# All attention scores of a head pair in one TensorE batch, two more jobs that ScalarE may take, and new TensorE prices in the planner

## The chip, the cores and the metric

One core of a Trainium2 chip. The metric is the device time of one launch in microseconds (us). The kernel before took 643.71 us, median of three runs (640.93 to 644.32). Engines in the profile: PE is TensorE's matmuls, PEld its weight loads, DVE is VectorE, ACT ScalarE, POOL GpSimd, SP the queue that issues the DMAs.

## The reference, cut to what matters

```python
# q, k, v: (2, 8, 768, 64) f32; n_sink = 4, window = 128
scores = q @ k.T / sqrt(64)
keep   = (key < n_sink) | (0 <= query - key < window)
a      = softmax(where(keep, scores, -1e9))
x      = (a @ v), heads side by side          # 1536 tokens x 512
h = maximum(x @ moe_w_in, 0);  x = (h * h) @ moe_w_out        # 512 -> 2048 -> 512
h = x @ moe2_w_in;  out = (h * sigmoid(1.702 * h)) @ moe2_w_out
```

Everything is float32, and n_sink and window are data that the kernel reads.

## The kernel before, in words

**Attention.** Queries go in 6 groups of 256 and, in each, 4 pairs of heads: 24 pairs, one call of `Attn.pair` each. A group has four blocks of 64 queries; block n sees 128 + 64 keys of its window and 8 sink keys, `KB` = 200 columns. `pair` goes over w = 0 and 1 (two blocks each). For each w, `mm_quarters` (L397) issues the scores as 64x64 tiles of the TensorE array, two blocks by two heads, into columns 0 to 200 of the PSUM banks a0 and a1 (one per head). Then, per head, VectorE adds the mask and takes the maximum (L765), and ScalarE takes the exponential with its sum (L767). The batch of w = 1 writes the same columns as that of w = 0, so it waits until VectorE has read both banks. In the first group of a batch element the batch of w = 0 has 136 columns (`cuts`). The transposes (L418) of the probabilities, the product with v as 128x64 or 64x64 tiles (`mm_halves`, L411) and two more transposes make a slice of x, which is split into a high and a low float32r part.

**The two layers.** Each goes over 16 blocks of 128 hidden units and over 3 tiles of 512 tokens (in attention's time, over 256 tokens: groups 0 to 3, three blocks of layer 1). A step is `first` (12 matmuls, L392), `act`, `second` (12 matmuls). For 512 tokens that is 24 matmuls of 512 columns. In layer 1 `act` has ScalarE take the relu of the PSUM bank into r (L564), VectorE multiply the bank by r in place (`tt`, L369), ScalarE copy it into gh (L351) and VectorE subtract gh (L369).

**Weights.** They arrive as 64-bit words and are decoded in pieces of 128x512, two for each of 32 blocks (`decode`). A piece takes on VectorE a range check (L479: the smallest absolute value, kept in a column of `least`), two shifts and masks (L482, L487), two combinations (L483, L489) and a mask (L491); on ScalarE a scaling (L485) and a copy (L351); and a multiplication on VectorE or GpSimd (L369, L370). 11 blocks are kept in SBUF: 7 from the start, 4 more when attention has given back its space. `make_flag` tests `least` at the end.

**The order.** Nothing is issued in the order of the text. Every operation is added to a `Plan` with a price in ns, what it reads and what it writes, and with a price for each engine that may take it (`choose`). `solve` plays six rounds of a list schedule with these prices, with `LAG` between engines, a model of TensorE's clock (`Clock`) and weights per engine (`PRICE`, ScalarE 1.2 and VectorE 1.5 per ns), keeps the shortest, and `emit` writes the instructions in that order. On the chip each engine then works through its own list in order. While there is nothing else for TensorE at the start, the plan puts matmuls of zeros there (L857).

Of the kernel before, what the change touches and what calls it, by code (L numbers as in the profile page):

```python
# [9 lines left out]
F32 = mybir.dt.float32  # L10
# [274 lines left out]
def kernel(  # L285
# [59 lines left out]
    def in_psum(*aps):  # L345
        return any(t.space == bass.MemoryType.PSUM for t in aps)
# [19 lines left out]
    def tt(engs, o, a, b, op, reads=(), writes=(), wide=0):  # L366
        n = o.free_size()
        every = {
            "V": ((100 if in_psum(a, b) else 69) + 1.04 * n, lambda: nc.vector.tensor_tensor(o, a, b, op)),  # L369
            "P": (145 + (2.11 + wide) * n, lambda: nc.gpsimd.tensor_tensor(o, a, b, op)),  # L370
        }
        ps = in_psum(o, a, b)
        choose([e for e in engs if not (e == "P" and ps)], every, not in_psum(a, b), reads, writes)
# [4 lines left out]
    def vec(ns, fn, reads=(), writes=(), port=False):  # L378
        step("V", ns, fn, reads, writes, port=port)
# [7 lines left out]
    def mm(calls, reads, writes):  # L387


        def fn():  # L390
            for o, a, b, start, stop in calls:
                nc.tensor.matmul(o, a, b, start=start, stop=stop)  # L392

        ns = lambda n, dt: max(107, (1 if dt == F32R else 4) * n / 2.4 + 2.5)
        step("E", sum(ns(c[2].free_size(), c[2].dtype) for c in calls), fn, reads, writes, calls[0][1].shape[0] / P)

    def mm_quarters(calls, n, reads, writes):  # L397


        def fn():  # L400
            for o, a, b, start, stop in calls:
                nc.tensor.matmul(o, a, b, start=start, stop=stop)  # L402

        step("E", 4 * n / 2.4 + 70, fn, reads, writes, 0.8)

    def mm_halves(calls, reads, writes):


        def fn():
            for o, a, b, start, stop in calls:  # L410
                nc.tensor.matmul(o, a, b, start=start, stop=stop)  # L411

        step("E", sum(2 * c[2].free_size() / 2.4 + 8 for c in calls) + 60, fn, reads, writes, 0.8)

    def transposes(calls, reads, writes):
        def fn():
# [8 lines left out]
    lim = T(cpool, [P, 2], F32, "lim")  # L425
    lim_hi = T(cpool, [P, 2], F32, "lim_hi")
    ns_f, win_f = lim[:, 0:1], lim[:, 1:2]
    least = T(cpool, [P, 4 * NF], F32, "least")
    flag_f = T(cpool, [P, 3], F32, "flag_f")
    flag_i = T(cpool, [P, 1], I32, "flag_i")  # L430

# [10 lines left out]
    def make_flag():  # L442

        a, b = flag_f[:, 0:1], flag_f[:, 1:2]

        def fn():
            nc.vector.tensor_scalar(a, ns_f, float(NS), None, ALU.is_gt)
            nc.vector.tensor_scalar(b, win_f, 1.0, None, ALU.is_lt)
            nc.vector.tensor_tensor(a, a, b, ALU.max)
            nc.vector.tensor_scalar(b, win_f, float(P), None, ALU.is_gt)  # L450
            nc.vector.tensor_tensor(a, a, b, ALU.max)
            nc.vector.tensor_reduce(b, least, AX.X, ALU.min)
            nc.vector.tensor_scalar(b, b, LEAST_HI, None, ALU.is_lt)
            nc.vector.tensor_tensor(a, a, b, ALU.max)

        def last():
            nc.vector.tensor_reduce(flag_f[0:1, 2:3], banks["a2"][0:1, 0:P], AX.X, ALU.max)
            nc.vector.tensor_copy(flag_i[0:1], flag_f[0:1, 2:3])

        vec(900, fn, ["lim", "least"], ["flag"])  # L460
        transposes([(banks["a2"][0:1, 0:P], a)], ["flag"], ["a2"])
        vec(400, last, ["a2"], ["flag"])


    def decode(raw, rk, w, wk, least_col, scratch, keep):

        words = raw.bitcast(I32).rearrange("p (n t) -> p n t", t=2)  # L470
        lo, hi = words[:, :, 0], words[:, :, 1]
        kl, kh = (rk, "lo"), (rk, "hi")
        a, ka = scratch()
        if keep is not None:
            vec(600, lambda: nc.vector.tensor_scalar(a, hi, 0x7FFFFFFF, None, ALU.bitwise_and), [kh], [ka])
            vec(600, lambda: nc.vector.tensor_scalar(keep, fv(a), LEAST_HI, None, ALU.is_ge), [ka], ["keep"])
            tt("V", fv(hi), fv(hi), keep, ALU.mult, [kh, "keep"], [kh])
        else:
            vec(602, lambda: nc.vector.tensor_reduce(least_col, fv(hi), AX.X, ALU.min, apply_absolute_value=True),  # L479
                [kh], ["least"])  # L480

        vec(335, lambda: nc.vector.tensor_scalar(lo, lo, 9, None, ALU.logical_shift_right), [kl], [kl], True)  # L482
        vec(602, lambda: nc.vector.scalar_tensor_tensor(lo, hi, 23, lo, ALU.logical_shift_left, ALU.bitwise_or),  # L483
            [kh, kl], [kl], True)
        act(520, lambda: nc.scalar.activation(fv(lo), lo.bitcast(U32), AF.Copy, scale=2.0**-43), [kl], [kl])  # L485

        vec(335, lambda: nc.vector.tensor_scalar(a, hi, 0x07FFFE00, 3, ALU.bitwise_and, ALU.logical_shift_left),  # L487
            [kh], [ka], True)
        vec(602, lambda: nc.vector.scalar_tensor_tensor(a, hi, -0x40000000, a, ALU.bitwise_and, ALU.bitwise_or),  # L489
            [kh, ka], [ka], True)  # L490
        vec(335, lambda: nc.vector.tensor_scalar(hi, a, -0x800000, None, ALU.bitwise_and), [ka], [kh], True)  # L491
        copy(EN["dH"], w[0], fv(a), [ka], [(wk, "h")])
        tt(EN["dL"], w[1], fv(lo), fv(hi), ALU.mult, [kl, kh], [(wk, "l")], wide=0.3)


    class Moe:
# [25 lines left out]
        def decode(self):  # L522

            if self.n_dec == len(self.blocks):
                return
            blk = self.blocks[self.n_dec]
            t, wk = self.weights[self.n_dec % len(self.weights)]
            for mat in range(2):
                raw, rk = self.raw()
                dma(raw, w_dram[(blk[0], mat)][blk[1]], (), [(rk, "lo"), (rk, "hi")])  # L530
                n = 2 * self.n_dec + mat
                col = least[:, n : n + 1] if self.check else None
                decode(raw, rk, t[2 * mat : 2 * mat + 2], (wk, mat), col, self.scratch, self.keep)
            self.w[blk] = (t, wk)
            self.n_dec += 1

# [21 lines left out]
        def act(self, s):  # L558
# [6 lines left out]
            else:  # L565
                act(51 + 0.833 * n, lambda: nc.scalar.activation(r, ps, AF.Sigmoid, scale=GELU), [bank, "table"], [kr])  # L566

            tt("V", ps, ps, r, ALU.mult, [kr, bank], [bank])
            copy(EN["gh"], gh, ps, [bank], [kh])
            sub("V", gl, ps, fv(gh), [bank, kh], [kl])  # L570
            s["g"] = (gh, gl, kh, kl)
# [124 lines left out]
    class Attn:  # L696
# [27 lines left out]
        def pair(self, i):  # L724
# [13 lines left out]
            p, pk = self.p()  # L738
            st, stk = self.st()
            nm, sm, ri = (st[:, 4 * n : 4 * n + 4] for n in range(3))  # L740
            for w in range(2):
                cut = cuts[w]
                mask, mask_keys = self.masks[(first, w)]

                if w == 0:
                    parts = [(cut, KB - cut, [K_AT[u] + cut for u in range(2)])]
                else:
                    parts = [(0, P, [K_AT[u] + WIDE_AT[u] for u in (2, 3)]),
                             (P, KB - P, [K_AT[u] + REST_AT[u] for u in (2, 3)])]
                calls = []  # L750
                for dst, n, src in parts:
                    for b in range(2):
                        for h in range(2):
                            q = Q0 + (2 * w + b) * P + h * HQ
                            calls.append((
                                banks[BANKS["s"][h]][half(b), dst : dst + n], raw[half(h), q : q + HQ],
                                raw[half(h), K0 + src[b] : K0 + src[b] + n], True, True,
                            ))
                mm_quarters(calls, KB - cut, [(rk, "qk")], list(BANKS["s"]))
                for h in range(2):  # L760
                    n, one = KB - cut, slice(2 * w + h, 2 * w + h + 1)
                    pu = p[:, 2 * w + h, cut:]

                    vec(77 + 1.04 * n, lambda pu=pu, ps=banks[BANKS["s"][h]][:, cut:KB], mask=mask[:, cut:], one=one:
                        nc.vector.tensor_tensor_reduce(pu, ps, mask, -0.125, 3.0e38, ALU.add, ALU.min, nm[:, one]),  # L765
                        [BANKS["s"][h]] + mask_keys, [(pk, w, h), (stk, "nm", w, h)])
                    act(280 + 0.833 * n, lambda pu=pu, one=one: nc.scalar.activation(  # L767
                        pu, pu, AF.Exp, bias=nm[:, one], scale=-1.0, accum_out=sm[:, one]),
                        [(pk, w, h), (stk, "nm", w, h)], [(pk, w, h), (stk, "sm", w, h)])
# [54 lines left out]
    with ExitStack() as fast:  # L824
# [31 lines left out]
        early[0] = True  # L856
        plan[0].filler = lambda: nc.tensor.matmul(banks["h"][:, 0:P], zero, zero, start=True, stop=True)  # L857
        vec(100, lambda: nc.vector.memset(zero, 0.0), (), ["zero"])
        at.load()
        constants()  # L860
        at.masks = build_masks(sums[NTILE - 1].rearrange("p a b -> p (a b)"))
# [195 lines left out]
```

## Time and profile before

| | |
|---|---|
| median of the runs | 643.71 us |
| the profiled execution | 644.05 us, its span 642.1 us |
| PE busy | 625.8 us, 97% of the span |
| DVE / ACT / POOL busy | 445.2 (69%) / 281.1 (44%) / 35.3 us (6%) |
| mean granted clock of TensorE | 0.989 of full |

Busy shares are means over the span, and the kernel has two parts: attention with a little of layer 1 up to about 156 us, and the two layers alone after that. Matmuls overlap, so a matmul's "busy" is longer than its pace. What one costs where TensorE has a queue of work is the distance between the starts of neighbours.

### The profile page before, as it was taken

The page shows a single profiled execution, that of the slowest core. Times are in us where ns is not written, and L with a number is a line of the kernel's source. Part 1 is how long each engine was busy: PE and PEld are TensorE (multiplying, and loading weights), DVE is VectorE, ACT ScalarE, POOL GpSimd, SP SyncE. Part 2 cuts the span into 40 slices and gives each one's busy share as a digit, 9 for nine tenths or more (in the row PEclk, how much of TensorE's full clock was granted, in tenths as well). Part 3 has the DMA queues.
Part 4 walks back from the last instruction along what each step waited for, and adds up shares of the span by engine and source line. Part 5 has one row for each costly group of instructions (what it writes and reads, how often), then busy time and mean ns, then how long its engine had stood idle before and what let it go on. Part 6 is the DMA issues. An engine that isn't in the chain of part 4 may idle for free.

```text
span 642.1 us, 10443 instructions
## 1 busy us (share of the span) xinstructions
PE 625.8 (97%) x4039; PEld 517.2 (81%) x4039; DVE 445.2 (69%) x1040; ACT 281.1 (44%) x626; POOL 35.3 (6%) x45
## 2 busy tenths in 40 slices
PE   7999999998999999999999999999999999999995
PEld 6777778897888888888888888888888888888884
DVE  5898889988877889998888998522277651333313
ACT  4687677764533444353343544232444331221211
POOL 1010000001010010010020110000000000000000
PEclk7999899999999999999999999999999999999998
DMA  6686655323122112241131312100021200101001
GB/s 241 200 267 222 222 187 187 121 69 129 66 98 100 61 70 86 79 132 52 57 123 34 98 38 94 34 1 0 5 94 66 84 16 1 65 1 65 1 0 70
DMA packets 14744, 56.77 MB, mean 88 GB/s; under 512 B 1760, under 2 KB 1760, under 8 KB 14688
## 3 DMA queue, kind: packets, MB, share of 16 engines
q1 hardware_dynamic: 14688, 56.04, 26.2%
q8 instruction: 33, 0.54, 0.4%
q14 instruction: 23, 0.19, 0.1%
HBM read 52.89 MB, written 3.15 MB: 87 GB/s over the span
## 4 chain that ended last, share of the span: by engine, by line
PE 94%; DVE 2%; ACT 1%; DMA 1%; issue 0%; SPq 0%; ACTq 0%
PE c L392 41%; PE a L392 25%; PE h L392 15%; PE c L411 5%; PE a L402 3%; PE c L418 3%; PE a L418 2%; DMA ints<-in_limits_dram 1%; PE h L857 1%; DMA raw<-in_w_out_dram 1%; ACT p L767 0%; DVE sum L369 0%; ACT pw L351 0%; DVE pw L352 0%; DVE p L765 0%
## 5 line engine op out<-in xcount | busy, mean ns | idle before, releaser
L392 PE MATMUL a<-xh,w 128*128 128x512 f32 x480 | 156.9, 390 | 0.0
L392 PE MATMUL c<-w,ghw 128*128 128x512 f32 x384 | 118.4, 389 | 0.0
L392 PE MATMUL c<-ghw,w 128*128 128x512 f32 x336 | 107.2, 389 | 2.0 <-ACT ghw L351 2.0
L392 PEld LDWEIGHTS a<-xh,w 128*128 128x128 f32 x480 | 90.1, 188 | 18.7
L392 PE MATMUL h<-xh,w 128*128 128x512 f32 (+1 forms) x336 | 104.7, 366 | 0.0
L369 DVE TENSOR_TENSOR a<-a,rw 128x512 f32<-128x512 f32 x60 | 41.9, 698 | 76.4 <-ACT rw L566 65.2
L392 PE MATMUL a<-xl,w 128*128 128x512 f32 x240 | 93.4, 389 | 0.0
L392 PEld LDWEIGHTS c<-w,ghw 128*128 128x128 f32 x384 | 72.0, 188 | 15.0
L392 PEld LDWEIGHTS c<-ghw,w 128*128 128x128 f32 x336 | 63.1, 188 | 15.4 <-ACT ghw L351 2.5
L392 PE MATMUL c<-w,glw 128*128 128x512 f32 x192 | 74.7, 389 | 0.0
L392 PEld LDWEIGHTS h<-xh,w 128*128 128x128 f32 x336 | 62.3, 190 | 9.8 <-issue 0.3
L392 PE MATMUL c<-glw,w 128*128 128x512 f32 x168 | 65.5, 390 | 0.2 <-DVE glw L369 0.2
L485 ACT ACTIVATE raw<-raw 128x512 f32<-128x512 uint32 x64 | 43.2, 675 | 43.2 <-DVE raw L483 43.1
L392 PE MATMUL h<-xl,w 128*128 128x512 f32 (+1 forms) x168 | 60.5, 360 | 0.0
L369 DVE TENSOR_TENSOR glw<-a,ghw 128x512 fp32r<-128x512 f32 x60 | 41.2, 687 | 17.7 <-ACT ghw L351 16.6
L351 ACT ACTIVATE ghw<-a 128x512 fp32r<-128x512 f32 x60 | 36.0, 599 | 39.0 <-DVE a L369 35.0
L566 ACT ACTIVATE rw<-a 128x512 f32<-128x512 f32 x32 | 19.2, 599 | 76.9 <-PE a L392 76.5
L392 PEld LDWEIGHTS a<-xl,w 128*128 128x128 f32 x240 | 45.1, 188 | 9.2
L351 ACT ACTIVATE w<-dec 128x512 fp32r<-128x512 f32 x64 | 40.2, 631 | 19.8 <-DVE dec L489 17.2
L479 DVE TENSOR_REDUCE least<-raw 128x1 f32<-128x512 f32 x64 | 43.3, 677 | 6.8 <-DMA raw<-in_w_out_dram 6.6
L767 ACT ACTIVATE p<-p,st 128x200 f32<-128x200 f32 (+1 forms) x96 | 42.5, 448 | 7.4 <-DVE st L765 7.0
L370 POOL TENSOR_TENSOR w<-raw 128x512 fp32r<-128x512 f32 x21 | 22.8, 1087 | 411.8 <-DVE raw L491 300.4
(101 smaller groups left out, 907.1 us busy)
## 6 DMA issues: line engine op xcount, KB each, us to landing
raw<-in_w_in_dram SPq DMA_DIRECT2D x32, 512.0 KB, 3.9
raw<-in_w_out_dram SPq DMA_DIRECT2D x32, 512.0 KB, 3.5
qkv<-in_qkv_dram SPq DMA_DIRECT2D x16, 840.0 KB, 4.7
qkv<-in_qkv_dram SPq DMA_DIRECT2D x7, 680.0 KB, 5.2
out_dram<-sum SPq DMA_DIRECT2D x12, 256.0 KB, 2.1
qkv<-in_qkv_dram SPq DMA_DIRECT2D x1, 424.0 KB, 3.4
qkv<-in_qkv_dram SPq DMA_DIRECT2D x1, 256.0 KB, 6.8
ints<-in_limits_dram SPq DMA_DIRECT2D x1, 2.0 KB, 3.9
```

The lines of the kernel that those rows point to most:

```text
L351: "A": ((51 if ps else 94) + 0.833 * n, lambda: nc.scalar.activation(o, i, AF.Copy)),
L369: "V": ((100 if in_psum(a, b) else 69) + 1.04 * n, lambda: nc.vector.tensor_tensor(o, a, b, op)),
L370: "P": (145 + (2.11 + wide) * n, lambda: nc.gpsimd.tensor_tensor(o, a, b, op)),
L392: nc.tensor.matmul(o, a, b, start=start, stop=stop)
L402: nc.tensor.matmul(o, a, b, start=start, stop=stop)
L411: nc.tensor.matmul(o, a, b, start=start, stop=stop)
L418: nc.tensor.transpose(o, i, ident)
L479: vec(602, lambda: nc.vector.tensor_reduce(least_col, fv(hi), AX.X, ALU.min, apply_absolute_value=True), [kh], ["least"])
L485: act(520, lambda: nc.scalar.activation(fv(lo), lo.bitcast(U32), AF.Copy, scale=2.0**-43), [kl], [kl])
L566: act(51 + 0.833 * n, lambda: nc.scalar.activation(r, ps, AF.Sigmoid, scale=GELU), [bank, "table"], [kr])
L767: act(280 + 0.833 * n, lambda pu=pu, one=one: nc.scalar.activation(pu, pu, AF.Exp, bias=nm[:, one], scale=-1.0, accum_out=sm[:, one]), [(p ...
L857: plan[0].filler = lambda: nc.tensor.matmul(banks["h"][:, 0:P], zero, zero, start=True, stop=True)
```

## The change

- `pair` issues the scores of w = 0 and w = 1 in one batch (`mm_quarters` is called once, with 24 matmuls). Those of w = 1 go to columns 200 to 400 of the same banks. VectorE's four reads follow.
- `decode`'s range check may go to ScalarE: the absolute value into a scratch tile `junk`, then relu(LEAST_HI - |x|), whose sum is kept in a column of `below`. The plan chooses by price, 602 ns on VectorE or 1130 ns on ScalarE. `least` and `below` are set by GpSimd at the start, and `make_flag` tests `below` with three more VectorE instructions.
- In layer 1 the square may go to ScalarE: Square of r into the bank, for VectorE's multiplication of the bank by r.
- Prices: a matmul of n columns costs n/2.4 + 13.4 ns (before n/2.4 + 2.5), a score batch 180 ns beside its columns (before 70), a product with v 190 ns (before 60), a VectorE `tensor_tensor` 74 + 1.04n ns.

```diff
 def tt(...):
-            "V": ((100 if in_psum(a, b) else 69) + 1.04 * n, lambda: nc.vector.tensor_tensor(o, a, b, op)),
+            "V": (74 + 1.04 * n, lambda: nc.vector.tensor_tensor(o, a, b, op)),
 def mm(...):
-        ns = lambda n, dt: max(107, (1 if dt == F32R else 4) * n / 2.4 + 2.5)
+        ns = lambda n, dt: max(107, n / 2.4 + 13.4 if dt == F32R else 4 * n / 2.4 + 5)
 def mm_quarters(...):
-        step("E", 4 * n / 2.4 + 70, fn, reads, writes, 0.8)
+        step("E", 4 * n / 2.4 + 180, fn, reads, writes, 0.8)
 def mm_halves(...):
-        step("E", sum(2 * c[2].free_size() / 2.4 + 8 for c in calls) + 60, fn, reads, writes, 0.8)
+        step("E", sum(2 * c[2].free_size() / 2.4 + 8 for c in calls) + 190, fn, reads, writes, 0.8)
 def make_flag(): ...
+            nc.vector.tensor_reduce(b, below, AX.X, ALU.max)
+            nc.vector.tensor_scalar(b, b, 0.0, None, ALU.is_gt)
+            nc.vector.tensor_tensor(a, a, b, ALU.max)
 def decode(...):
-            vec(602, lambda: nc.vector.tensor_reduce(least_col, fv(hi), AX.X, ALU.min, apply_absolute_value=True),
-                [kh], ["least"])
+            def by_scalar():
+                nc.scalar.activation(junk, fv(hi), AF.Abs)
+                nc.scalar.activation(junk, junk, AF.Relu, bias=least_hi, scale=-1.0, accum_out=below_col)
+            every = {
+                "V": (602, lambda: nc.vector.tensor_reduce(least_col, fv(hi), AX.X, ALU.min, apply_absolute_value=True)),
+                "A": (1130, by_scalar),
+            }
+            choose("VA", every, False, [kh, "checks"], ["check"])
 def act(self, s):
-            tt("V", ps, ps, r, ALU.mult, [kr, bank], [bank])
+            every = {"V": (74 + 1.04 * n, lambda: nc.vector.tensor_tensor(ps, ps, r, ALU.mult))}
+            if s["layer"] == 1:
+                every["A"] = (69 + 0.833 * n, lambda: nc.scalar.activation(ps, r, AF.Square))
+            choose(list(every), every, False, [kr, bank], [bank])
 def pair(self, i):
+            for w, dst, n, src in (
+                (0, cuts[0], KB - cuts[0], [K_AT[u] + cuts[0] for u in (0, 1)]),
+                (1, 0, P, [K_AT[u] + WIDE_AT[u] for u in (2, 3)]),
+                (1, P, KB - P, [K_AT[u] + REST_AT[u] for u in (2, 3)]),
+            ):
+                for b in range(2):
+                    for h in range(2):
+                        q = Q0 + (2 * w + b) * P + h * HQ
+                        calls.append((
+                            banks[BANKS["s"][h]][half(b), w * KB + dst : w * KB + dst + n], raw[half(h), q : q + HQ],
+                            raw[half(h), K0 + src[b] : K0 + src[b] + n], True, True,
+                        ))
+            mm_quarters(calls, 2 * KB - cuts[0], [(rk, "qk")], list(BANKS["s"]))
             for w in range(2):
-                ...
-                mm_quarters(calls, KB - cut, [(rk, "qk")], list(BANKS["s"]))
                 for h in range(2):
-                    vec(77 + 1.04 * n, lambda pu=pu, ps=banks[BANKS["s"][h]][:, cut:KB], mask=mask[:, cut:], one=one:
+                    vec(77 + 1.04 * n, lambda pu=pu, ps=ps, mask=mask[:, cut:], one=one:
                     ...
+        def checks():
+            nc.gpsimd.memset(least, 1.0e30)
+            nc.gpsimd.memset(below, 0.0)
+            nc.gpsimd.memset(least_hi, LEAST_HI)
+        step("P", 450, checks, (), ["checks"])
```

## Rows read from the trace of the kernel before

**Rows 1.** The page: busy us, share and instructions by engine; granted clock in 40 slices.

```profile
PE 625.8 (97%) x4039; PEld 517.2 (81%) x4039; DVE 445.2 (69%) x1040; ACT 281.1 (44%) x626; POOL 35.3 (6%) x45
PEclk7999899999999999999999999999999999999998
```

**Rows 2.** Windows: stretch, its length, busy us of each engine, PEclk, DMA, GB/s.

```profile
14.00:75.50 61.50, 59.20 (x946) 46.81 (x944) 54.75 (x215) 46.29 (x158) 3.13 (x3) 1.00 0.67 217
75.50:79.00 3.50, 3.50 (x29) 3.12 (x19) 2.15 (x8) 1.51 (x6) 0.00 (x0) 0.53 0.72 253
79.00:146.00 67.00, 66.59 (x857) 56.86 (x857) 59.33 (x199) 47.67 (x141) 4.51 (x4) 1.00 0.43 148
146.00:156.00 10.00, 7.73 (x39) 6.09 (x38) 8.54 (x18) 5.87 (x13) 2.04 (x2) 1.00 0.23 63
156.00:632.60 476.60, 476.60 (x2104) 394.64 (x2104) 310.12 (x555) 173.79 (x290) 23.47 (x23) 1.00 0.17 57
632.60:642.10 9.50, 2.06 (x10) 1.36 (x8) 2.73 (x4) 0.00 (x0) 0.00 (x0) 0.83 0.33 118
```

**Rows 3.** Waits of PE from 14 to 156 us: us in total, times, longest.

```profile
PE c L392 <- ACT ghw L351: 2.0, 1, 2.0
PE c L411 <- DVE xl L369: 1.7, 3, 1.0
PE c L418 <- ACT p L767: 0.4, 1, 0.4
PE c L392 <- DVE glw L369: 0.2, 1, 0.2
```

**Rows 4.** Timeline of PE around three score batches (L402): start, us, instruction, count.

```profile
52.90 0.57 PE L402 MATMUL a<-qkv 64*64 64x200 f32 x8
53.40 0.44 PE L418 MATMUL c<-ident,xn 128*128 128x128 f32 x2
...
54.60 0.28 PE L392 MATMUL h<-xl,w 128*128 128x256 f32 x1
54.71 0.28 PE L392 MATMUL h<-xh,w 128*128 128x256 f32 x1
54.92 0.57 PE L402 MATMUL a<-qkv 64*64 64x128 f32 x16
55.43 0.34 PE L411 MATMUL c<-qkv,pr 72*64 72x64 f32 x4
...
71.30 0.46 PE L402 MATMUL a<-qkv 64*64 64x136 f32 x8
71.69 0.30 PE L418 MATMUL c<-ident,p 128*72 128x128 f32 x1
```

**Rows 5.** Lines by form, whole span: busy us, mean ns, idle before, releaser.

```profile
L479 DVE TENSOR_REDUCE least<-raw 128x1 f32<-128x512 f32 x64 | 43.3, 677 | 6.8 <-DMA raw<-in_w_out_dram 6.6
L369 DVE TENSOR_TENSOR h<-h,r 128x256 f32<-128x256 f32 x12 | 5.1, 429 | 1.3 <-ACT r L564 1.2
L485 ACT ACTIVATE raw<-raw 128x512 f32<-128x512 uint32 x64 | 43.2, 675 | 43.2 <-DVE raw L483 43.1
L351 ACT ACTIVATE w<-dec 128x512 fp32r<-128x512 f32 x64 | 40.2, 631 | 19.8 <-DVE dec L489 17.2 <-PE c L392 2.4
L767 ACT ACTIVATION_READ_ACCUMULATOR p<-p,st 128x1 f32 x96 | 18.5, 193 | 0.0
L564 ACT ACTIVATE r<-h 128x256 f32<-128x256 f32 x12 | 4.6, 380 | 7.0 <-PE h L392 7.0
L882 ACT ACT_TABLE_LOAD x1 | 1.3, 1283 | 0.0
```

**Rows 6.** The chain that ended last, 146 to 156 us: start, us, what.

```profile
146.42 3.41 DMA raw<-in_w_out_dram
...
151.22 0.59 DVE least L479
...
152.41 0.60 DVE least L479
```

More of the change, by code (lines that the diff above doesn't have):

```diff
@@ L427 @@
     ns_f, win_f = lim[:, 0:1], lim[:, 1:2]
-    least = T(cpool, [P, 4 * NF], F32, "least")
+    least, below = (T(cpool, [P, 4 * NF], F32, tag) for tag in ("least", "below"))
+    least_hi = T(cpool, [P, 1], F32, "least_hi")
+    junk = T(cpool, [P, DM], F32, "junk")
     flag_f = T(cpool, [P, 3], F32, "flag_f")
@@ L458, in last, with decode @@
             nc.vector.tensor_copy(flag_i[0:1], flag_f[0:1, 2:3])
-        vec(900, fn, ["lim", "least"], ["flag"])
+        vec(1300, fn, ["lim", "check"], ["flag"])
         transposes([(banks["a2"][0:1, 0:P], a)], ["flag"], ["a2"])
         vec(400, last, ["a2"], ["flag"])
-    def decode(raw, rk, w, wk, least_col, scratch, keep):
+    def decode(raw, rk, w, wk, least_col, below_col, scratch, keep):
         words = raw.bitcast(I32).rearrange("p (n t) -> p n t", t=2)
@@ L531, in decode @@
                 n = 2 * self.n_dec + mat
-                col = least[:, n : n + 1] if self.check else None
-                decode(raw, rk, t[2 * mat : 2 * mat + 2], (wk, mat), col, self.scratch, self.keep)
+                decode(raw, rk, t[2 * mat : 2 * mat + 2], (wk, mat), least[:, n : n + 1], below[:, n : n + 1],
+                       self.scratch, self.keep)
             self.w[blk] = (t, wk)
@@ L740, in pair @@
             nm, sm, ri = (st[:, 4 * n : 4 * n + 4] for n in range(3))
+            calls = []
+            for w, dst, n, src in (
[11 more added lines that the diff above has]
+            mm_quarters(calls, 2 * KB - cuts[0], [(rk, "qk")], list(BANKS["s"]))
             for w in range(2):
@@ L743, in pair @@
                 mask, mask_keys = self.masks[(first, w)]
[L745 to L758, printed above, removed]
-                mm_quarters(calls, KB - cut, [(rk, "qk")], list(BANKS["s"]))
                 for h in range(2):
                     n, one = KB - cut, slice(2 * w + h, 2 * w + h + 1)
-                    pu = p[:, 2 * w + h, cut:]
-                    vec(77 + 1.04 * n, lambda pu=pu, ps=banks[BANKS["s"][h]][:, cut:KB], mask=mask[:, cut:], one=one:
+                    pu, ps = p[:, 2 * w + h, cut:], banks[BANKS["s"][h]][:, w * KB + cut : (w + 1) * KB]
+                    vec(77 + 1.04 * n, lambda pu=pu, ps=ps, mask=mask[:, cut:], one=one:
                         nc.vector.tensor_tensor_reduce(pu, ps, mask, -0.125, 3.0e38, ALU.add, ALU.min, nm[:, one]),
```

## The prediction, made before the changed kernel was run

> **What bounds the kernel now.** I read the page's engine table and clock first, then windows, then TensorE's waits, then its timeline around single batches, and the prices of lines last. The table says TensorE 97%, VectorE 69% [rows 1], but that is a mean over two different parts, so the windows count [rows 2]. From 156.0 to 632.6 us TensorE runs 2104 matmuls in 476.6 us, 226.5 ns each, with no gap: only fewer or cheaper matmuls would shorten that stretch, and the change alters none of them. VectorE has 310 of 477 us there and ScalarE 174, so work that moves between these two is hidden behind TensorE in that part, at nothing; the cover is 167 us of idle VectorE and 303 us of idle ScalarE. The last 9.5 us are the last matmuls, four VectorE sums and the stores; nothing in the change touches them. What is left is the part before 156 us.
>
> There TensorE is also the one with a queue of work. From 14 to 146 us (the first three windows) VectorE is busy 54.75 + 2.15 + 59.33 = 116.2 of 132 us (88%) and ScalarE 46.29 + 1.51 + 47.67 = 95.5 us (72%) [rows 2]. TensorE's own waits from 14 to 156 us add up to only 2.0 + 1.7 + 0.4 + 0.2 = 4.3 us [rows 3]. So in attention TensorE's issue time sets the pace, with VectorE close behind, and TensorE time that goes there comes off the end. Two losses stand beside it: 3.4 us at half clock (0.53 of full in 75.5 to 79.0, that is 1.2 in place of 2.4 GHz), 2 us after TensorE's longest wait for VectorE (1.0 us, [rows 3]), which costs 1.7 us; and 146 to 156 us, where TensorE is busy 7.7 of 10 us.
>
> **The change part by part.**
>
> *One batch in place of two.* The price of a batch comes from three of them [rows 4]. A batch of 200 columns starts at 52.90 and the next instruction at 53.40: 0.50 us. One of 136 columns takes from 71.30 to 71.69: 0.39 us. So 64 columns cost 0.11 us, 1.72 ns a column; 200 columns stream in 0.344 us, and 0.156 us of a batch is fixed. The batch of w = 1, which has its 200 columns in 16 matmuls of 128 and 72 columns, takes 54.92 to 55.43, 0.51 us: more matmuls within the same tiling cost 0.01, so the fixed part belongs to the batch and not to its matmuls. Getting in costs too: matmuls of 256 columns stand 0.11 apart (54.60, 54.71), but 0.21 before the batch (54.71, 54.92), so 0.10 more. Each batch less saves 0.156 + 0.095 = 0.25 us. There are 24 pairs with one batch less each: 24 x 0.25 = 6.0 us. Bounds: 0.16 us if the entry is hidden by a longer queue (3.7 us), and 0.3 if the pause for the banks goes too (7.2 us); I take 6.0, the measured sum.
>
> *The wait for the banks.* Today the batch of w = 1 waits for two reads by VectorE and the next pair's first batch for two more; afterwards one batch waits for four. What is queued behind a waiting batch on TensorE is all that the plan put after it: transposes, products with v and layer matmuls. The loop is then about 1.0 us of batch, four reads of at most 0.43 us (VectorE's 256-column form [rows 5]) and two hand-overs, about 3 us, against (146 - 14) / 24 = 5.5 us of a pair's period today, so it does not bind. Value: nothing; up to 0.1 us a pair (2.4 us) lost if the plan puts the batch too close behind the reads, up to the 1.7 us of waits for VectorE gained.
>
> *The range check.* On VectorE 0.677 us a piece [rows 5]; 22 pieces belong to the 11 blocks decoded by about 156 us, 14.9 us. ScalarE's form isn't in the trace. The nearest rows: the absolute value reads the same strided words as L485 (0.675), the relu is like L351 from SBUF (0.631), its sum read-out like L767's (0.193): 1.50 us, against 1.13 in the plan; as a low bound the plan's 1.13. All 22 would put ScalarE at 95.5 + 33 = 128.5 us in a stretch of 126: they cannot all go. The plan weighs 1.2 x 1130 = 1356 against 1.5 x 602 = 903, so ScalarE gets a check only where it could begin 0.45 us earlier. I take a third, 7: VectorE -4.7, ScalarE +10.5 us.
>
> *The square.* VectorE 0.429 us on 256 columns, ScalarE about the 0.380 of its relu [rows 5]; of 12 in attention I take half: VectorE -2.6, ScalarE +2.3. Together VectorE has 116.2 - 4.7 - 2.6 = 109 and ScalarE 95.5 + 10.5 + 2.3 = 108 us in 126, 87% each: they remain under TensorE. If nothing moved, VectorE would be at 116 / 126 = 92%. The rows alone make ScalarE the dearer engine for the check (1.50 against 0.677) and the cheaper one for the square (0.380 against 0.429). The Trainium skill speaks against both: "ScalarE: Activation LUTs" (Rules for kernel authors) wants relu and multiplications on VectorE and not on ScalarE; the rows agree for the check and not for the square, and what it would cost here is a rival below.
>
> *The prices.* The new price of a 512-column matmul, 512/2.4 + 13.4 = 226.7 ns, is what the trace has (226.5); the old one gave 215.8. The plan now knows TensorE's pace and the 0.25 us around a batch. That orders the other engines' work by later and truer due times. Of the 4.3 us of waits I count 1 us as gone, with bounds of +4 (a new order with waits of its own) and -4.3 us. The wait at the end of attention is the largest (2.0 + 0.2): the chain there goes from a weight DMA of 3.41 us through the decoding on VectorE, two range checks of 0.6 us among it [rows 6], to the first 512-column step; two checks on ScalarE would take up to 1.2 us off it.
>
> *Small parts.* Three more instructions for the flag and three GpSimd memsets lie in time that these engines idle (POOL has 35 us of work in the whole span); nothing. At the start, the second scores come sooner, but their masks don't: nothing, within 1 us either way. The half-clock stretch I leave as it is: 1.7 us to gain if TensorE waits less, as much to lose if a wait comes elsewhere.
>
> **Sum.** Span 642.1 - 6.0 - 1.0 = 635.1; the profiled execution took 1.95 us more than its span, so 637.0. That execution (644.05) stands 0.3 above the median of 643.71, so against the median I say 637.0 as well, 6.7 us or 1.0% less. The likeliest case's own range: 633.5 to 640.4.
>
> **The rivals.**
>
> *VectorE takes over* (0.19). Its 116 us of work, in order, have 16 us of idle in 132, and if these are unavoidable hand-overs, VectorE keeps the pace, and TensorE's 6 us turn into waits: 641 to 646, 644 in the middle. For it: the longest waits of TensorE are on VectorE [rows 3]. Against it: they are short and few, and both new choices can only take work off VectorE.
>
> *ScalarE in the way* (0.10, slower). ScalarE works in order, and a check of 1.5 us, priced at 1.13, in front of an exponential delays the transposes, the product with v and the next layer step. From 0.25 x 24 / 1.5 = 4 checks of the 22 that lie fully on TensorE's path the gain is gone; with 8 it is 644 + 6 = 650. Against it: 28% of ScalarE is idle in that stretch. The rule of the Trainium skill cited above points to this case.
>
> *A table for Square* (0.04, slower). A table load takes 1.283 us, and the line that brings in the sigmoid's has one [rows 5]; if Square or Abs needed another table than the exponential, 12 squares in attention would bring up to 24 loads, 31 us on ScalarE: 95.5 + 31 is more than the stretch, some 5 us over, so about 644 + 5 = 649. The Trainium skill, "ScalarE: Activation LUTs" (Table sets: the hidden batching unit), names relu, copy, identity and abs as filler of every set, and not Square; no row here shows a Square.
>
> *The plan clears its waits* (0.12). Batches 6.0, waits 4.3, the half clock 1.7: 632 and below to about 630. The chain of 146 to 156 us speaks for it, the fixed order on engines with jitter against it.
>
> **How the numbers follow.** Forecast 0.55. A change of under 0.5% (3.2 us) can't be told from none here: faster means below 640.5, slower above 646.9. Faster: 0.55 + 0.12 = 0.67; same: 0.19; slower: 0.10 + 0.04 = 0.14. The range of 631.5 to 645.5 takes the forecast's own, half of the case below it and most of VectorE's: about 0.8.
>
> **What would show it.** One score batch of 24 matmuls a pair, lasting about 2 x 0.344 + 0.16 = 0.85 us to the next instruction, 24 of them in place of 48. The stretch without gaps then begins about 149 us in place of 156, at 226.5 ns a matmul as before. VectorE's share before it falls, ScalarE's rises; some checks (an Abs and a Relu) and Squares appear on ScalarE, with no further table load. Wrong would be: a batch of 1.1 us (the fixed part went with the columns); the saving turned into waits for VectorE or ScalarE before 150 us; gaps after it; or the batches back at two.

## The result, and the profile after

The changed kernel takes 637.65 us (median of 7 runs, 636.66 to 639.38), the kernel before, run beside it, 644.32 us (640.93 to 645.7): ratio 0.9903, 95% interval 0.988 to 0.9925. Forecast: 637.0, in 631.5 to 645.5. The profiled span went from 642.1 to 635.7 us, 6.4 us less.

The page after (engines and granted clock, as in [rows 1]):

```profile
PE 619.5 (97%) x4033; PEld 516.8 (81%) x4033; DVE 401.6 (63%) x974; ACT 343.8 (54%) x771; POOL 36.8 (6%) x50
...
PEclk8999999999999999999999999999999999999998
```

Windows of the kernel after, columns as in [rows 2]; the first four answer to the first four there:

```profile
14.00:75.50 61.50, 59.29 (x970) 51.01 (x968) 56.86 (x227) 53.39 (x174) 3.12 (x3) 1.00 0.66 228
75.50:79.00 3.50, 3.50 (x54) 3.02 (x46) 3.33 (x14) 2.78 (x10) 0.00 (x0) 1.00 0.88 322
79.00:146.00 67.00, 64.36 (x813) 57.26 (x809) 57.81 (x186) 55.70 (x156) 8.57 (x7) 1.00 0.46 155
146.00:156.00 10.00, 10.00 (x46) 8.29 (x45) 7.02 (x15) 6.95 (x13) 0.00 (x0) 1.00 0.39 137
...
128.60:144.30 15.70, 13.63 (x103) 11.59 (x103) 12.34 (x24) 11.84 (x25) 3.43 (x3) 1.00 0.31 102
144.30:626.10 481.80, 480.70 (x2112) 395.56 (x2111) 274.53 (x501) 226.54 (x411) 22.00 (x21) 1.00 0.17 55
626.10:635.70 9.60, 2.92 (x13) 2.07 (x12) 2.84 (x5) 0.00 (x0) 0.00 (x0) 0.78 0.33 118
```

The long stretch of layers begins at 144.3 us in place of 156, and the last part is as long as before (9.6 against 9.5 us). From 75.5 to 79.0 us the clock is now at full. VectorE's total fell by 43.6 us and ScalarE's rose by 62.7: the checks that moved are dearer on ScalarE.

Two score batches of the kernel after (timeline of PE, the rows that answer to [rows 4]): one with 200 columns for w = 0 and one with 136. The trace has two records for each float32 matmul, so the 24 of a batch are the 12 matmuls that the program issues.

```profile
119.97 0.28 PE L392 MATMUL h<-xh,w 128*128 128x256 f32 x1
120.09 0.60 PE L418 MATMUL c<-ident,p 128*72 128x128 f32 x4
120.52 0.60 PE L418 MATMUL a<-ident,p 128*128 128x128 f32 x4
121.05 0.91 PE L402 MATMUL a<-qkv 64*64 64x200 f32 x24
121.89 0.34 PE L411 MATMUL c<-qkv,pr 72*64 72x64 f32 x4
...
16.73 0.81 PE L402 MATMUL a<-qkv 64*64 64x136 f32 x24
17.46 0.44 PE L418 MATMUL c<-ident,xn 128*128 128x128 f32 x2
```

From 121.05 to 121.89 is 0.84 us, for which two batches took 0.50 + 0.51, and one entry of 0.10 is gone as well. The median over the 24 batches is 0.843 us, measured from a batch's first matmul to the next instruction's; of the 48 before it was 0.504.

TensorE's waits in the whole kernel after (us, times, longest; [rows 3] are those of before up to 156 us):

```profile
PE a L402 <- DMA qkv<-in_qkv_dram: 3.3, 3, 2.4
PE c L392 <- ACT ghw L351: 2.0, 2, 1.7
PE h L872 <- DVE zero L873: 1.1, 1, 1.1
PE c L392 <- DVE glw L369: 1.1, 4, 0.4
PE c L411 <- DVE xl L369: 1.1, 3, 0.5
```

One is new: score batches that wait for the DMA of q, k and v, 2.4 us of it at the start, the rest in attention.

What ScalarE took over up to 146 us, and the checks that stayed on VectorE (L490) (lines by form: busy us, mean ns | idle before):

```profile
L487 ACT ACTIVATE junk<-junk,least_hi 128x512 f32<-128x512 f32 x9 | 6.5, 723 | 0.4
L490 DVE TENSOR_REDUCE least<-raw 128x1 f32<-128x512 f32 x9 | 6.1, 681 | 1.0 <-DMA raw<-in_w_out_dram 1.0
L486 ACT ACTIVATE junk<-raw 128x512 f32<-128x512 f32 x9 | 6.1, 680 | 3.7 <-DMA raw<-in_w_out_dram 2.1 <-DMA raw<-in_w_in_dram 1.6
L583 ACT ACTIVATE h<-r 128x256 f32<-128x256 f32 x10 | 3.8, 384 | 0.2
L487 ACT ACTIVATION_READ_ACCUMULATOR junk<-junk,least_hi 128x1 f32 x9 | 1.7, 186 | 0.0
L351 ACT ACT_TABLE_LOAD x1 | 1.3, 1283 | 0.7 <-PEq L1069 0.7
L904 ACT ACT_TABLE_LOAD x1 | 1.3, 1283 | 0.0
```

Nine checks of 0.680 + 0.723 + 0.186 = 1.59 us and ten squares of 0.384 us; two table loads in all, as before.

### The profile page after: what moved, and what is told of

Its sections match the earlier page's. It is cut to its first block, busy times and chain, and to the rows that moved or that the text cites. A ratio compares the mean times of both kernels' runs of the same rounds, so it can differ in the third digit from the quotient of the medians.

```text
span 635.7 us, 10424 instructions
## 1 busy us (share of the span) xinstructions
PE 619.5 (97%) x4033; PEld 516.8 (81%) x4033; DVE 401.6 (63%) x974; ACT 343.8 (54%) x771; POOL 36.8 (6%) x50
## 4 chain that ended last, share of the span: by engine, by line
PE 61%; DVE 17%; DMA 14%; ACT 5%; issue 2%; POOL 1%; SPq 0%; DVEq 0%; POOLq 0%; ACTq 0%
PE c L392 27%; PE a L392 16%; PE h L392 9%; DMA raw<-in_w_out_dram 8%; PE c L411 3%; DMA qkv<-in_qkv_dram 3%; DMA raw<-in_w_in_dram 3%; PE a L402 2%; DVE raw L496 2%; DVE dec L502 2%; PE c L418 2%; DVE glw L369 1%; DVE raw L495 1%; DVE sum L369 1%; DVE dec L500 1%
## 5 line engine op out<-in xcount | busy, mean ns | idle before, releaser
L392 PE MATMUL a<-xh,w 128*128 128x512 f32 x480 | 158.8, 389 | 0.0
L392 PE MATMUL c<-ghw,w 128*128 128x512 f32 x336 | 108.5, 390 | 1.7 <-ACT ghw L351 1.7
L392 PE MATMUL h<-xh,w 128*128 128x512 f32 (+1 forms) x336 | 103.4, 363 | 0.0
L581 DVE TENSOR_TENSOR a<-a,rw 128x512 f32<-128x512 f32 x40 | 27.9, 697 | 65.1 <-ACT rw L579 64.9
L502 DVE SCALAR_TENSOR_TENSOR dec<-raw,dec 128x512 int32<-128x512 int32 x64 | 43.9, 690 | 0.0
L496 DVE SCALAR_TENSOR_TENSOR raw<-raw 128x512 int32<-128x512 int32 x64 | 43.7, 683 | 0.0
```

What stands on the lines that cost most here:

```text
L581: every = {"V": (74 + 1.04 * n, lambda: nc.vector.tensor_tensor(ps, ps, r, ALU.mult))}
```

## The experiments

The theory is that of the prediction: the 0.25 us around a score batch is TensorE's own time for the change of tiling, and attention runs at TensorE's pace. The rivals: the new prices made a better order; or VectorE was the pace and ScalarE relieved it. The change has three parts that can be had one by one, so all eight combinations were timed: before, after and six more (each against the kernel before on its own chip).

**One batch alone, and everything but the batch.** The first is the kernel before with `pair` of after; the second is after with `pair` of before:

```diff
 # everything but the batch: after, with the loop of before
             for w in range(2):
                 ...
+                mm_quarters(calls, KB - cut, [(rk, "qk")], list(BANKS["s"]))
```

> The kernel before with the scores of both w in one batch and nothing else of the change (old prices, no new jobs for ScalarE). Theory (the 0.25 us around a batch is TensorE's own time and attention runs at TensorE's pace): 24 x 0.25 = 6.0 us less than before, 638 to 639. Rival, the new prices: the gain comes from a better order, so the batch alone changes nothing, 643 to 645. Rival, VectorE: attention runs at VectorE's pace and the gain comes from what ScalarE took over, again 643 to 645 here.

> The changed kernel with two score batches a pair as before; new prices and ScalarE's new jobs stay. Theory: the 6.0 us come back, 643 to 644. Rival prices and rival VectorE: most of the gain stays, 638 to 640.

One batch alone: 636.08 us, ratio 0.9875 (0.984 to 0.9909), 8.2 us less than the 644.29 beside it and no worse than the whole change. Everything but the batch: 646.95 us, 1.0051 (1.0028 to 1.0073), slower than before. Both rivals fall, and the other two parts bring nothing here. Both times also miss the theory's range, by 2 to 3 us and toward a larger effect (638 to 639 and 643 to 644 were expected); part of that goes with the granted clock, as shown below the table. The price of a batch in the kernel with one batch alone is the same as in after (median 0.843 us). Its waits are not:

```profile
PE c L411 <- DVE xl L369: 4.5, 7, 1.2
PE a L402 <- DVE st L764: 2.9, 2, 2.5
PE a L402 <- DMA qkv<-in_qkv_dram: 2.0, 3, 1.1
```

Products with v wait 4.5 us for VectorE in place of 1.7 [rows 3]: a faster TensorE does come closer to VectorE, but these waits are far from the size of the saving.

**Prices alone, ScalarE's jobs alone, and each left out.** Edits: the old or new prices in `tt`, `mm`, `mm_quarters`, `mm_halves`; ScalarE as a choice or not (the kernel with one batch and prices keeps the memsets and flag instructions of after):

```diff
-            choose("VA", every, False, [kh, "checks"], ["check"])
+            choose("V", every, False, [kh, "checks"], ["check"])
...
-            if s["layer"] == 1:
+            if False:
                 every["A"] = (69 + 0.833 * n, lambda: nc.scalar.activation(ps, r, AF.Square))
```

> The kernel before with the new prices alone: two batches a pair, no new jobs for ScalarE. One batch alone gave 636.1 us and everything but the batch 647.0, so prices and ScalarE's jobs together cost 2 to 3 us. Theory P (the prices do it: another order with waits of its own): 645.5 to 647. Theory S (ScalarE's jobs do it, since a check takes longer there than its price): 643 to 645, no change.

> The kernel before with ScalarE's two new jobs alone: two batches, old prices. Theory S: 645.5 to 647. Theory P: 643 to 645, or less where VectorE is relieved.

> The changed kernel without ScalarE's two new jobs: one batch and new prices. Theory S: as one batch alone, 635.5 to 637. Theory P: as the changed kernel, 637.5 to 639.

> The changed kernel with the old prices: one batch and ScalarE's two new jobs. Theory P: as one batch alone, 635.5 to 637. Theory S: as the changed kernel, 637.5 to 639.

| one batch | prices | ScalarE's jobs | us | ratio to before (95%) | DVE busy us | of it 14 to 146 us | median granted clock |
|---|---|---|---|---|---|---|---|
| | | | 644.3, 643.9 | 1 | 445 | 116.2 | 0.990, 0.993 |
| | x | | 641.81 | 0.9978 (0.9954 to 1.0002) | 440 | 114.6 | 0.9925 |
| | | x | 645.02 | 1.004 (1.0009 to 1.0071) | 404 | 110.9 | 0.993 |
| | x | x | 646.95 | 1.0051 (1.0028 to 1.0073) | 403 | 108.4 | 0.9875 |
| x | | | 636.08 | 0.9875 (0.984 to 0.9909) | 443 | 115.2 | 0.994 |
| x | x | | 639.39 | 0.9942 (0.9918 to 0.9966) | 436 | 118.1 | 0.990 |
| x | | x | 637.70 | 0.9919 (0.9889 to 0.9949) | 406 | 112.1 | 0.991 |
| x | x | x | 637.65 | 0.9903 (0.988 to 0.9925) | 402 | 118.0 | 0.994 |

One batch saves in each of the four comparisons: 8.2, 2.4, 7.3 and 9.3 us, mean 6.8. The prices give -2.1, +3.3, +1.9 and -0.1 us, mean +0.8. ScalarE's jobs give +1.2, +1.6, +5.1 and -1.7, mean +1.6. So neither part has an effect of one sign, and neither theory fits all four runs: P misses with prices alone (641.81 for 645.5 to 647), S with ScalarE's jobs left out (639.39 for 635.5 to 637) and, by half a us, with them alone (645.02 for 645.5 to 647).

VectorE's 30 to 40 us less buy no gain that repeats, but most of them lie in the two layers, where VectorE has time to spare. Between 14 and 146 us ScalarE's jobs take 5.3, 6.2, 3.1 and 0.1 us from VectorE, and the times go by +1.2, +5.1, +1.6 and -1.7 us. So this answers the rival VectorE for 3 to 6 us of relief, not for 40. What answers it as a whole is one batch alone, which leaves VectorE its work (115.2 us for 116.2) and gains 8.2 us.

The spread of 2.4 to 9.3 us is the scatter of the contexts: any edit to what the planner sees gives a new order. Part of it goes with the granted clock. Of the 73 executions of the kernel before beside the runs of this section, the 25 at 0.995 or more have a median of 641.6 us and the 34 at 0.989 to 0.991 one of 644.3. The smallest saving stands where the kernel with one batch had the lower clock (0.990 against 0.9925), the largest where it had the higher one (0.994 against 0.9875). At 2.7 us per 0.005 of clock, an estimate from these executions, the four become about 6.0, 3.8, 8.4 and 5.8, mean 6.0. What in a plan makes the rest was not found.

**The tiling change by itself.** After's order and prices; the first kernel puts a small matmul of zeros inside each score batch, the second puts it ahead of a pair's first transposes, which are 128x128 like the zeros:

```diff
 # inside the batch (mm_quarters)
-            for o, a, b, start, stop in calls:
+            for i, (o, a, b, start, stop) in enumerate(calls):
+                if i == 4:
+                    nc.tensor.matmul(banks["a0"][:, 400:432], zero, zero[:, 0:32], start=True, stop=True)
                 nc.tensor.matmul(o, a, b, start=start, stop=stop)
 # the control (ahead of a pair's first transposes)
+                nc.tensor.matmul(ps_r[:, 0:32], zero, zero[:, 0:32], start=True, stop=True)
```

> The changed kernel, same order and prices, with one 128x128 matmul of zeros (32 columns, into columns of the bank that no score uses) between the scores of w = 0 and w = 1. It splits the batch by a change of the array's tiling and adds no wait on another engine. Theory: 24 times 0.25 us for the second entry and fixed part, plus the matmul itself (between 0.03 and 0.11 us, or 1 to 2.6 us in all): 645 to 646. Rival (the fixed part of a batch was a hand-over with VectorE and not the tiling): only the matmul itself, 638.5 to 640.

> The control for the split batch: the same matmul of zeros, 24 times, but ahead of a pair's first transposes, where the array stays in its 128x128 tiling. Both theories: 1 to 2.6 us more than the changed kernel, 638.5 to 640. The difference between the two is the price of the tiling change alone: 6 us by the theory, none by the rival.

Split: 645.25 us (1.0013, 0.999 to 1.0035). Control: 640.2 us (0.9939, 0.9915 to 0.9963). The difference is 5.05 us, 0.21 us a batch, where the theory said 6 and its rival none; the median granted clock is alike (0.9935 and 0.993). A split batch in the timeline of the first, then the zeros in the control:

```profile
106.23 0.57 PE L404 MATMUL a<-qkv 64*64 64x200 f32 x8
106.73 0.41 PE L403 MATMUL a<-zero 128*128 128x32 f32 x2
107.07 0.57 PE L404 MATMUL a<-qkv 64*64 64x128 f32 x16
107.57 0.34 PE L413 MATMUL c<-qkv,pr 72*64 72x64 f32 x4
```

```profile
107.16 0.30 PE L418 MATMUL c<-zero 128*128 128x32 f32 x2
107.30 0.39 PE L420 MATMUL c<-ident,p 128*72 128x128 f32 x2
```

From 106.23 to 107.57 is 1.34 us for what takes 0.84 unsplit: 0.50 more, against 0.14 for the same zeros in the control (0.03 to 0.11 was expected). The batch contains no wait on another engine that the unsplit one lacks, so this is TensorE's own time. The control is less clean than its expectation says. Of its places after the first pair, 11 stand between 128x128 matmuls, at 0.14 us each, but 12 stand right behind a score batch or products with v, and there the next instruction starts 0.24 us after the zeros (0.45 once, at half clock). So the change of tiling alone is worth between 24 x (0.50 - 0.24) = 6.2 and 24 x (0.50 - 0.14) = 8.6 us on TensorE; 5.05 of them reach the end. A 64x64 matmul of zeros inside the batch, an interruption without a change of tiling, was not run; that 16 records of one tiling take 0.01 us more than 8 for the same columns [rows 4] speaks against the interruption as the cause.

**The same rule at the products with v.** In the 8 pairs of a first group `mm_halves` alternates between 128x64 and 64x64 tiles. Putting its two 64-row matmuls side by side halves these changes. It was tried on after and on one batch alone:

```diff
+            if first:
+                (r00, r01, w0, r10, r11, w1), more = calls[:6], calls[6:]
+                calls = [r00, r10, r11, w1, (*w0[:3], True, False), (*r01[:3], False, True), *more]
             mm_halves(calls, [prk, (pwk, 0), (pwk, 1), (rk, "v")], [ok])
```

> The changed kernel; in the 8 pairs of a first group the products with v are reordered so that the two 64-row matmuls stand together: the tiling changes twice within the batch in place of four times. There 28 matmuls took 1.66 us, and 32 of one tiling take 1.08. 28 of one tiling would be 0.95, so a change costs 0.71 / 4 = 0.18 us. Theory (a change of the tiling is TensorE time wherever it stands): 8 x 2 x 0.18 = 2.9 us less if all is on the path, 634.7 to 637; rival (in the first groups TensorE waits for data anyway): 637.5 to 638.5.

> One batch alone (old prices, nothing new on ScalarE) with the same reordering of the products with v. Theory: 636.1 - 2.9 = 633.2, to 635; rival (hidden by waits for data): 635.5 to 637.

638.13 us (0.9927, 0.9901 to 0.9953) and 635.66 us (0.9893, 0.9867 to 0.992): each the same as without the reordering, and each where its rival put it. The products of such a pair in the chain, after and then reordered (start, us, count):

```profile
19.22 1.66 PE c L411 x28
```

```profile
18.40 1.47 PE c L411 x28
```

0.19 us less, not the 0.36 expected: I had put the whole of 1.66 - 0.95 down to the four changes of tiling and divided by four. 8 x 0.19 = 1.5 us on TensorE is under the scatter of the plans, and whether it reaches the end isn't shown.

**A fifth buffer for q, k and v.** One batch alone, without and with the reordering:

```diff
-BUFS = dict(raw=2, dec=2, qkv=4, p=4, st=4, pw=2, pr=3, xn=2, r=2, gh=3, gl=2)
+BUFS = dict(raw=2, dec=2, qkv=5, p=4, st=4, pw=2, pr=2, xn=2, r=2, gh=3, gl=2)
```

> One batch alone with five buffers for q, k and v in place of four (and, for the space, two for pr in place of three). With one batch, and only then, TensorE waits for the DMA of q, k and v, 2.0 us in the profile of one batch alone. Theory (that wait is the ring's depth): it goes, 634 to 635.5. Rival (the DMA itself is late, or the wait turns up elsewhere, or pr with two buffers makes one): 636 to 638.

> One batch, the reordered products with v and five buffers for q, k and v (two for pr). Theory: both gains add up, 631.5 to 633.5; rival (each hides behind the same waits for VectorE): 634 to 636.

636.11 us (0.9903, 0.9879 to 0.9927), unchanged; and 634.34 us (0.9881, 0.9852 to 0.991), the lowest of all. Some of TensorE's waits in the first, then in the second:

```profile
PE c L411 <- DVE xl L369: 3.0, 5, 1.2
PE a L402 <- DMA qkv<-in_qkv_dram: 2.5, 2, 2.3
...
PE c L418 <- DVE xn L369: 1.2, 1, 1.2
```

```profile
PE c L411 <- DVE xl L369: 3.0, 5, 1.2
PE a L402 <- DVE st L764: 2.7, 1, 2.7
PE c L392 <- ACT gh L351: 1.2, 2, 1.0
PE c L418 <- DVE xn L369: 1.2, 1, 1.2
```

Of the DMA waits 0.2 us is left beside the 2.3 at the start, and new ones stand beside them (1.2 us on ScalarE's gh, 1.2 on VectorE's xn), with the time unchanged: the rival's outcome. At the start the two profiles differ in what came last for the same batch (DMA or VectorE, 2.3 and 2.7 us). The last kernel lies in its rival's range (634 to 636), and its interval overlaps those of after and of one batch alone; the two edits can't be told from the scatter.

## Why the prediction was right, point by point

- *TensorE's issue time sets the pace of attention.* Shown: one batch saves in all four comparisons, zeros that split a batch cost 5.05 us more than the same zeros outside it, and taking 3 to 6 us from VectorE in attention brought no gain. Not every us of TensorE reaches the end, though: the split adds 24 x 0.50 = 12 us to after on TensorE and 7.6 us (637.65 to 645.25) to its time.
- *One batch, 24 x 0.25 = 6.0 us.* Right in mechanism and size. In the trace after it is 0.50 + 0.51 - 0.84 + 0.10 = 0.27 us a pair, 6.5 us. The predicted batch of 0.85 us measured 0.84. In time the four comparisons have a mean of 6.8 us, about 6.0 at like clock.
- *The wait for the banks: nothing.* Among TensorE's waits of after from 14 to 150 us no score batch waits more than 0.2 us for VectorE. What I did not name is the wait for q, k and v: with one batch a pair's whole q and k are wanted at once and pairs follow sooner. It is among TensorE's waits in every profile with one unsplit batch and four buffers (1.2 to 4.9 us) and in none with two batches; 0.9 of its 3.3 us in after lies beyond 14 us.
- *The range check.* I took 7 of 22 on ScalarE at 1.50 us; up to 146 us it was 9 of 18, at 1.59 us. The 22 was too many: the trace of before has 17 checks up to 156 us. VectorE has 56.86 + 3.33 + 57.81 = 118.0 us from 14 to 146 us, 89%, where I said 87% of a shorter stretch. The work that left was replaced: 18 pieces are begun by 146 us where it was 15, and the plan put 10 of the 24 casts of x to xh on VectorE where it was 2. So "both new choices can only take work off VectorE" was wrong.
- *The square.* 10 of 12 on ScalarE, where I took half, at 0.384 us for an estimated 0.380. No table load beside the two: the rival of a table for Square is out. In that rival's sum, 95.5 + 31 us is 0.5 over the 126, not 5. The rule of the Trainium skill ("ScalarE: Activation LUTs", Rules for kernel authors), which prefers VectorE for multiplications and gives its figure for bf16, does not hold for this float32 square, 0.384 us on ScalarE and 0.426 to 0.429 on VectorE; for the check it does, 1.59 against 0.681 us.
- *The prices, 1 us of waits gone.* This term failed: TensorE's waits are 4.7 us from 14 to 150 us, where they were 4.3 [rows 3]. Those at the end of attention are where they were: TensorE is idle 15.7 - 13.6 = 2.1 us from 128.6 to 144.3, as 10.0 - 7.7 = 2.3 us were idle before [rows 2]. The chain there is again a weight DMA, 4.39 us at 131.99, and decoding behind it, now with a check on ScalarE in it:

```profile
131.99 4.39 DMA raw<-in_w_out_dram
...
136.46 0.72 ACT junk L486
...
137.21 0.82 ACT junk L487 x2
138.02 0.58 ACT raw L498
```

  1.5 us of this chain is the check that VectorE had done in 0.6 [rows 6]: I had said that ScalarE would shorten this chain, and for this check it lengthens it.
- *Sum.* Up to the last product with v, less the layer matmuls done by then (0.227 us for a matmul of 512 columns, 0.120 for one of 256), the kernel after is 8.8 us ahead in the trace (98.0 against 106.8). Of this 6.5 is the batches and 1.7 the half clock at 75.5 to 79.0 us, which I had left as it is. 2.4 us are given back later, 1.1 of them in gaps of the long stretch, which had none before (481.80 us with TensorE busy 480.70); I had named gaps as a sign of being wrong. That stretch begins at 144.3 us, where I said 149, with 8 more matmuls in it than before. So -7.0 forecast and -6.4 measured are near each other in part by luck: the waits did not fall, and two terms that I had at nothing, the clock and the later gaps, have opposite signs. The executions show the size of the clock's part: at a granted clock of 0.995 or more the kernel before takes 641.6 us. Against that, after, with a median clock of 0.994, is 4.0 us less, and one batch alone, at 0.994 too, 5.5.
- *The rivals.* VectorE takes over: no, but it is close (4.5 us of waits in one batch alone). I had argued for it that the longest waits of TensorE are on VectorE; the longest in [rows 3] is 2.0 us, on ScalarE. ScalarE in the way: not in after, whose waits for it are 2.0 us in all. Everything but the batch, 1.0051, is 2.7 us slower, and ScalarE's jobs alone 1.2 us; that it is exponentials held up by checks is not shown. For the first the clock is as likely a cause: its profile has 0.56 of full clock for 13.6 us (7.8 to 21.4), where before has 0.52 for 6.8 us (7.2 to 14.0). The plan clears its waits: no; the half clock in attention went, the waits stayed.

## What to carry to other kernels

A change of the TensorE array's tiling has a price on TensorE itself, which the distance between starts shows and the busy share hides: count batches, take the price from two batches of different length, and merge what shares a tiling. Relief for an engine counts only in the stretch where that engine is close to the path: of 40 us taken from VectorE at most 6 lay there, and they bought nothing. Where a planner makes the order, one edit's effect is known to its scatter only (here some 3 us, part of it the granted clock), so time the part in several contexts, and compare executions of like clock, before believing a gain of that size.

## What the runs showed of the hardware that was not expected

A 64x64 batch split by one 128x128 float32 matmul of 32 columns (two records) costs 0.50 us more; the same matmul costs 0.14 between matmuls of its own tiling. Taking away two of four changes between 128x64 and 64x64 tiles saved only 0.19 us in 1.66 us.
